# Moving GpSimd's elementwise work to VectorE in a retention + two-FFN kernel, with the second layer's loads and operands re-timed

## The chip, the cores and the metric

One core of a Trainium2 chip runs the whole program. The metric is the device time of one execution in microseconds, as the median of several runs. Engines are named as in the profile: PE (TensorE matmul), PEld (its weight load), DVE (VectorE), ACT (ScalarE), POOL (GpSimd), SP (SyncE, which issues nearly all transfers here).

## What is computed

The reference is a retention layer (attention without softmax, with a decay mask), followed by two feed-forward layers:

```
scores = scale * q @ k^T                 # 4 batches, 8 heads, 576 positions, head size 64
ret    = (scores * Dmat) @ v             # Dmat[h, i, j] = gamma_h ** (i - j) for i >= j, else 0
x      = tokens(ret)                     # 2304 tokens x 512
h = x @ w_in;  x = max(0.01 * h, h) @ w_out     # layer 1, inner size 2048
h = x @ w_in2; out = (h * cos(h)) @ w_out2      # layer 2, inner size 2048
```

## The kernel before

**Precision.** Each fp32 operand is held as a high part (rounded by ACT) and a low part (the rest, a subtraction on DVE or POOL), and each product is made of three matmuls. The weights arrive as 64-bit words and are converted by ACT and DVE.

**Retention** runs over 18 chunks of 128 tokens. For a chunk `i`: `load_chunk(i)` (SP), `scale_q(i)` and `scale_v(i)` (elementwise, 128x512), `scores(i)` (PE, L255), `masks(i)` (DVE, L271), `values(i)` (PE, L286 and L300), `states(i)` (DVE, L318 and L320), `reads(i)` (PE, L333), `take(i)` (ACT, L359). Chunks alternate between two buffers, so chunk `i + 2` is loaded after `reads(i)`.

**Layer 1** runs over five blocks of tokens (512, 512, 512, 384, 384) and 16 tiles `f` of the inner size. A step issues `H(j, f)` on PE (`h_mm`, L456), and, two steps late (`LAG = 2`), `O(j, f)` (`o_mm`, L470). Between the two the result goes through ACT, ACT and DVE (L737, L741, L744). The chunks of block `j + 1` are worked on between the steps of block `j`. The block's input is split into high and low by `split_block` (ACT L675, DVE L679) once the last `H` of the block before has read the old one.

**Block 0** is written out by hand, and every engine takes its instructions in the order of the text. In the same steps DVE converts the layer's weights: in step `s` it does `conv_b` and `conv_c` for the weight tile two steps ahead (L402, L404, L408, L415) and, between them, `low_of(s + 1)` (L427), the low half of the next step's weight tile. Tiles 0 to 14 are converted whole, tile 15 in two halves. At the end of the step come

```
            if i is not None:
                reads(i)
                take(i)
                load_chunk(i + 2)
                if i + 2 >= n_busy:
                    scale_q(i + 2)
                    scale_v(i + 2)
```

with `n_busy` = 8. Chunks 4 to 7 are read in steps 4, 7, 10 and 13, so chunks 8 and 9 are loaded and scaled at the end of steps 10 and 13. They are first used in block 1.

**Blocks 1 to 4 and layer 2** are put in order by a planner (`Plan`): each task has an engine, an estimated time, what it needs and a due time; the planner plays the tasks through and writes each engine's instructions in the order that it found. On the chip each engine keeps to that order and waits where a task isn't ready. During blocks 1 to 4 the second layer's operands are made and stored in DRAM: weights by `second_weights` (converting, L931 to L942; sums, L837; splits, L816 and L820) and the tokens' combinations by `x_parts` (load L856, four sums on L837, four splits on L816 and L820). For token blocks 1 and 2 of layer 2, `x_parts` runs while layer 2 already does block 0.

**Layer 2** uses seven products in place of eight for 2x2 blocks. 24 units `u`; in each PE does `i_mm` (L1056) for `m` in the order 1, 5, 6, 2, 7, 3, 4 and, interleaved and later, `out_` (L1185). Results of `m` = 1 and 6 are copied by ACT from bank to bank (L1158); `gate` makes h * cos(h) with five DVE and five ACT steps (L1085 to L1122).

`low_switch` hands the memory of the first `EARLY` weight tiles to the second layer and begins its loads, `open_all` hands over the rest after the last `O`.

Of the kernel before, what the change touches and what calls it, by code (L numbers as in the profile page):

```python
# [19 lines left out]
P = 128  # L20
# [20 lines left out]
FIRST_CHUNK = 4  # L41
EARLY = 6

# [31 lines left out]

LATE, DRAIN = 12, 6
N_G, N_WO, N_H = 16, 4, 6

# [5 lines left out]
class Plan:  # L84
# [4 lines left out]
    def __init__(self):  # L89
        self.tasks = []  # L90
        self.rings = {}

    def add(self, eng, ns, emit, needs=(), due=0.0, lands=0, frees=()):

        self.tasks.append([eng, ns, emit, needs, due, lands, frees])
        return len(self.tasks) - 1

    def taken(self, ring, size):

        tiles = self.rings.setdefault(ring, [])  # L100
        old = tiles[-size] if len(tiles) >= size else []
        tiles.append([])
        return old, tiles[-1]

    def play(self):
        n = len(self.tasks)
        after = [[] for _ in range(n)]
        left = [0] * n
        for t, task in enumerate(self.tasks):
            for d in {*task[3], *task[6]} - {None}:  # L110
                after[d].append(t)
                left[t] += 1
        ready = [0.0] * n
        free = {}
        open_ = {t for t in range(n) if not left[t]}
        order = []
        self.began = {}
        while open_:

            def begins(t):  # L120
                return max(ready[t], free.get(self.tasks[t][0], 0.0))
# [3 lines left out]
            eng, ns, _, _, _, lands, _ = self.tasks[t]  # L125
            start = begins(t)
            free[eng] = start + ns
            open_.remove(t)
# [23 lines left out]
def retention_ffn_ffn(  # L152
# [67 lines left out]
    def scale_q(i):  # L220
        q = ch_t[i][:, 0]

        eng = nc.vector if i < n_busy else nc.gpsimd
        eng.tensor_tensor(out=q, in0=q, in1=itab_sb, op=ALU.mult)

    def scale_v(i):
        c = i % CYCLE * H
        if i in (1, 2) or n_first <= i < n_busy:
            for h in range(H):
                v = ch_t[i][:, 3, h * D : (h + 1) * D]  # L230
                nc.scalar.activation(v, v, AF.Copy, scale=vtab_sb[:, c + h : c + h + 1])
            return
        v3 = ch_t[i][:, 3].rearrange("p (h d) -> p h d", h=H)
        t3 = vtab_sb[:, c : c + H].unsqueeze(2).to_broadcast([P, H, D])
        eng = nc.gpsimd if i else nc.vector
        eng.tensor_tensor(out=v3, in0=v3, in1=t3, op=ALU.mult)
# [307 lines left out]
    def rest():  # L544
# [53 lines left out]
        for s in range(NF, len(steps) + LAG):  # L598
            i = chunk_at.get(s)
            o = steps[s - LAG]  # L600
            if s < len(steps):
                slots.append(("H", *steps[s]))
                if i is not None:
                    slots.append(("values", i))
                if s + 1 in chunk_at:
                    slots.append(("scores", chunk_at[s + 1]))
            if o[0]:
                slots.append(("O", *o))
            if i is not None:
                slots.append(("reads", i))  # L610
# [44 lines left out]

        SOON = 1000.0
        ACT = {128: 300, 256: 400, 384: 510, 512: 625}
        DVE = {128: 250, 256: 420, 384: 560, 512: 690}
        POOL = {256: 700, 512: 1320}

        def dma(ns, emit, needs, due, frees=()):
            return add("SP", ns, emit, needs, due, 2500, frees)

# [4 lines left out]
        def split_block(j, due):  # L668
            x_ready[j] = []
            n = TB[j]  # L670
            for p in range(KK):
# [10 lines left out]

                a = add("ACT", ACT[n], x_high, [x_use.get((j - 1, p)), *taken[j]], due + p / 100 - SOON)
                x_ready[j].append(add("DVE", DVE[n], x_low, [a], due + p / 100 - SOON))

# [35 lines left out]
        def ffn_h(slot):  # L721
# [28 lines left out]
            t = add("ACT", ACT[n], high, [t], due - SOON / 2, 0, g.old)  # L750
            t = add("DVE", DVE[n], lower, [t], due - SOON / 2)
            y.users.append(t)
# [26 lines left out]
        def chunk(i):  # L779
            due = at["scores", i]  # L780
            if i not in scaled:
                t = dma(2800, lambda: load_chunk(i), read_of[i - 2], due - 12)
                a = add("POOL", POOL[512], lambda: scale_q(i), [t], due - 4)
                b = add("POOL", POOL[512], lambda: scale_v(i), [t], due - 2)
                scaled[i] = [a, b]
# [22 lines left out]

        def split(src, buf, n, to_high, to_low, needs, due, eng="POOL"):

# [18 lines left out]
            h_ = add("ACT", ACT[n], high, needs, due, 0, old)  # L829
            l_ = add(eng, (POOL if eng == "POOL" else DVE)[n], lower, [h_], due)  # L830
            t = dma(1400 * n // 512, store, [l_], due)
# [7 lines left out]
        def sums(eng, first, ops, frees, due, n=256):  # L839
# [3 lines left out]
            for x, op in enumerate(ops):  # L843
                t = [add(eng, (POOL if eng == "POOL" else DVE)[n], lambda op=op: less(e, *op), t, due, 0, frees if not x else ())]
            return t[0]
# [3 lines left out]
        def x_parts(n, q, due, early_=True):  # L849

            bufs, got = (s_ring.next(), s_ring.next()) if early_ else tuple(Use(b) for b in pair_buf), []
            for l in range(2):
# [18 lines left out]
            made = sums(  # L871
                "POOL", got[0] + got[1],
                [(t1, b12, b11, sub_), (t2, b22, t1, sub_), (t3, b22, b12, sub_), (t4, b21, t2, sub_)],
# [21 lines left out]
        def w_sums(p, a11, a12, a21, a22, got, due):  # L895
# [4 lines left out]
            made = sums(  # L900
                "POOL", got,
                [(s1, a21, a22, ALU.add), (s2, s1, a11, sub_), (s3, a11, a21, sub_), (s4, a12, s2, sub_)],
# [15 lines left out]
        def convert(f, c, tb, due, old):  # L918
# [28 lines left out]
            a2 = add("ACT", 430, lambda: nc.scalar.mul(lo().bitcast(I32), lo(), 2.0**-29), [t], due)  # L947
            t = add("DVE", 330, lambda: both(3), [a1], due)
            t = add("DVE", 330, lambda: both(4), [t], due)
            t = add("DVE", 450, lambda: both(5), [t], due)  # L950
            t = add("DVE", 450, lambda: both(6), [t, a2], due)
            rb.users.append(t)
# [45 lines left out]
        def open_low():  # L998
# [5 lines left out]
            some(pool, "ws", [P, 2, 4, 2 * P], F32R, ws_ring.bufs)  # L1004
            some(pool, "wo", [P, 2, 2, DM], F32R, wo_ring.bufs[:3])

# [21 lines left out]

        def add_weights(u):
            p = u % NPAIR  # L1030
            for kind, ring, src, ns in (
                ("a", wa_ring, wa_d, 2100), ("s", ws_ring, ws_d, 2800), ("o", wo_ring, wo_d, 2800),
            ):
                b = w_buf[kind, u] = ring.next()
                w_task[kind, u] = dma(
                    ns, lambda b=b, src=src: nc.sync.dma_start(b.ap.bitcast(F32), src[p]),
                    [opened["all" if kind == "o" and u == 3 else "low"], *w_there[kind, p]],
                    unit_at(u) - (16 if kind != "o" else 4), b.old,
                )
# [3 lines left out]
        def add_x(n):  # L1043
            for x, m in enumerate(ORDER):
                b = x_now[m] = Use(x_buf[m])
                x_task[n, m] = dma(
                    2100, lambda m=m, b=b: nc.sync.dma_start(b.ap.bitcast(F32), xq_d[n][:, X_OF[m]]),
                    [opened["low"], *parts_done[n]], unit_at(NPAIR * n) - 12 + x, b.old,
                )
# [26 lines left out]
        def gate(u, m, due):  # L1076
# [27 lines left out]

            t = add("DVE", 560, rest_a, [t], due, 0, rb.old)
            t = add("DVE", 560, rest_b, [t], due)
            nb.users.append(t)
# [7 lines left out]

            t = add("DVE", 560, times, [t], due)
            rb.users.append(t)
# [7 lines left out]

            t = add("DVE", 560, lower, [t], due)
            hb.users.append(t)
# [126 lines left out]
        for slot in slots:  # L1254
# [3 lines left out]
            if slot == ("O", NB - 1, NF - 1):  # L1258
                first_banks()
                opened["all"] = add("-", 0, open_all, [*busy["a"], *busy["b"], opened["low"]], 0)  # L1260
        for _, _, fn in flows:
# [163 lines left out]
```

## Time and profile before

| | |
|---|---|
| median of 3 runs | 884.04 us (882.31 to 887.03) |
| profiled execution | 880.0 us, of which the span of the instructions is 878.2 us |
| busy: PE, PEld | 848.1 us (97%), 777.7 us (89%) |
| busy: DVE, ACT, POOL | 581.3 us (66%), 519.2 us (59%), 194.4 us (22%) |
| mean granted TensorE clock | 0.988 |

Retention's start and the first weights take the first 40 to 60 us; layer 1 runs to 493 us, layer 2 from there to 874.5 us. A timeline row gives start, length, engine, line, operation, output and inputs, count and, in brackets, how long the engine was idle before it and what ended that.

### The profile page before, as it was taken

The page shows a single profiled execution, that of the slowest core. Times are in us where ns is not written, and L with a number is a line of the kernel's source. Part 1 is how long each engine was busy: PE and PEld are TensorE (multiplying, and loading weights), DVE is VectorE, ACT ScalarE, POOL GpSimd, SP SyncE. Part 2 cuts the span into 40 slices and gives each one's busy share as a digit, 9 for nine tenths or more (in the row PEclk, how much of TensorE's full clock was granted, in tenths as well). Part 3 has the DMA queues.
Part 4 walks back from the last instruction along what each step waited for, and adds up shares of the span by engine and source line. Part 5 has one row for each costly group of instructions (what it writes and reads, how often), then busy time and mean ns, then how long its engine had stood idle before and what let it go on. Part 6 is the DMA issues. An engine that isn't in the chain of part 4 may idle for free.

```text
span 878.2 us, 16385 instructions
## 1 busy us (share of the span) xinstructions
PE 848.1 (97%) x6288; PEld 777.7 (89%) x6288; DVE 581.3 (66%) x1015; ACT 519.2 (59%) x1112; POOL 194.4 (22%) x177
## 2 busy tenths in 40 slices
PE   6699999999999999999999999999999999999998
PEld 6577888777787887989999999999999999999998
DVE  5799975566674557454721377888787776765772
ACT  4687764454555445445632478686778665777650
POOL 0000021453435436363320123413323000000000
PEclk8799999999999999999999999999999999999999
DMA  9915422655557665754469486989999398474311
GB/s 362 417 58 203 178 74 84 217 180 191 176 175 240 192 216 165 247 174 163 174 242 416 139 283 191 321 303 395 311 315 324 134 373 318 150 273 180 132 48 73
DMA packets 91950, 193.31 MB, mean 220 GB/s; under 512 B 7648, under 2 KB 55264, under 8 KB 81632
## 3 DMA queue, kind: packets, MB, share of 16 engines
q1 hardware_dynamic: 91728, 191.92, 62.2%
q8 instruction: 49, 0.80, 0.4%
q10 hardware_dynamic: 144, 0.35, 0.1%
q14 instruction: 29, 0.24, 0.1%
HBM read 143.22 MB, written 49.02 MB: 219 GB/s over the span
## 4 chain that ended last, share of the span: by engine, by line
PE 71%; DVE 12%; DMA 9%; ACT 4%; issue 2%; POOL 1%; SPq 1%; DVEq 0%; ACTq 0%; POOLq 0%
PE psum L1185 19%; PE psum L470 17%; PE psum L456 16%; PE psum L1056 15%; DMA raw<-in_w 2%; DMA mraw<-in_w 2%; PE psum L333 2%; DVE g L1122 1%; DMA wo<-more 1%; DVE r L1096 1%; DMA ws<-mt 1%; DVE r L1101 1%; PE psum L255 1%; DMA ch<-in_qkv 1%; PE psum L286 1%
## 5 line engine op out<-in xcount | busy, mean ns | idle before, releaser
L456 PE MATMUL psum<-x_sb,w 128*128 128x512 f32 (+1 forms) x960 | 218.2, 376 | 6.7 <-DVE x_sb L679 2.8
L1185 PE MATMUL psum<-g,wo 128*128 128x384 f32 x1152 | 222.4, 334 | 0.0
L470 PE MATMUL psum<-g,w 128*128 128x512 f32 (+1 forms) x960 | 215.3, 373 | 0.3 <-ACT graw L700 0.3
L456 PEld LDWEIGHTS psum<-x_sb,w 128*128 128x128 f32 x960 | 176.9, 191 | 34.1 <-DVE x_sb L679 4.6
L1185 PEld LDWEIGHTS psum<-g,wo 128*128 128x128 f32 x1152 | 201.7, 188 | 0.0
L470 PEld LDWEIGHTS psum<-g,w 128*128 128x128 f32 x960 | 173.9, 188 | 24.8 <-ACT graw L700 0.6
L1056 PE MATMUL psum<-x,ws 128*128 128x384 f32 x576 | 115.1, 335 | 4.4 <-ACT psum L1158 4.4
L1056 PEld LDWEIGHTS psum<-x,ws 128*128 128x128 f32 x576 | 100.8, 188 | 6.3 <-ACT psum L1158 6.3
L744 DVE TENSOR_TENSOR g<-graw,g 128x512 fp32r<-128x512 f32 (+1 forms) x64 | 44.2, 691 | 80.8 <-ACT g L741 80.6
L1056 PE MATMUL psum<-x,wa 128*128 128x384 f32 x432 | 86.3, 334 | 0.2 <-DVE h L1085 0.2
L1122 DVE TENSOR_TENSOR g<-h,g 128x384 fp32r<-128x384 f32 x96 | 60.4, 630 | 26.8 <-ACT g L1119 26.5
L1056 PEld LDWEIGHTS psum<-x,wa 128*128 128x128 f32 x432 | 75.9, 188 | 0.5 <-DVE h L1085 0.5
L1112 DVE SCALAR_TENSOR_TENSOR h<-r,h 128x384 f32<-128x384 f32 x96 | 55.6, 580 | 27.0 <-ACT r L1109 26.7
L741 ACT CAST g<-graw 128x512 fp32r<-128x512 f32 (+1 forms) x64 | 36.1, 564 | 57.2 <-PE psum L470 56.9
L1096 DVE SCALAR_TENSOR_TENSOR r<-n,h 128x384 f32<-128x384 int32 x96 | 59.0, 615 | 13.2 <-ACT n L1093 12.6
L1108 ACT ACTIVATE r<-r 128x384 f32<-128x384 f32 x96 | 50.5, 526 | 28.5 <-DVE r L1101 28.0
L737 ACT ACTIVATE graw<-psum 128x512 f32<-128x512 f32 (+1 forms) x64 | 34.7, 542 | 47.9 <-PE psum L456 47.7
L1101 DVE SCALAR_TENSOR_TENSOR r<-n,r 128x384 f32<-128x384 int32 x96 | 58.2, 607 | 1.7
L1093 ACT ACTIVATE n<-h 128x384 int32<-128x384 f32 x96 | 49.3, 519 | 11.6 <-DVE h L1085 11.2
L1119 ACT CAST g<-h 128x384 fp32r<-128x384 f32 x96 | 49.1, 512 | 10.5 <-DVE h L1112 10.3
L1109 ACT ACTIVATE r<-r 128x384 f32<-128x384 f32 x96 | 50.4, 525 | 2.0
L837 POOL TENSOR_TENSOR m<-m 128x256 f32<-128x256 f32 x24 | 22.0, 935 | 122.2 <-DMA m<-y 121.8
(81 smaller groups left out, 936.9 us busy)
## 6 DMA issues: line engine op xcount, KB each, us to landing
ws<-ws SPq DMA_DIRECT2D x24, 1024.0 KB, 7.0
wo<-wo SPq DMA_DIRECT2D x24, 1024.0 KB, 5.6
wa<-wa SPq DMA_DIRECT2D x24, 768.0 KB, 6.6
ch<-in_qkv SPq DMA_DIRECT2D x17, 1024.0 KB, 7.0
mraw<-in_w SPq DMA_DIRECT2D x64, 256.0 KB, 3.4
x<-xq SPq DMA_DIRECT2D x21, 768.0 KB, 8.8
raw<-in_w SPq DMA_DIRECT2D x15, 1024.0 KB, 10.0
xq<-m SPq DMA_DIRECT2D x84, 128.0 KB, 4.5
```

Of the source, the lines that this page charges most:

```text
L456: nc.tensor.matmul(hp, wt[:, i, cols], x_t[lj, k][:, j, :n], start=(k == 0 and a == 0), stop=(k == KK - 1 and a == 2),)
L470: nc.tensor.matmul(psum[:, BANK_O + m, :n], wt[:, i, cols], gt[:, j, :n], start=(f == 0 and a == 0), stop=(f == NF - 1 and a == 2),)
L1056: nc.tensor.matmul(bank[BANKS[m]], a[:, hl, i, j * P : (j + 1) * P], x[:, j, v, :], start=m in (1, 5) and j == 0 and n == 0, stop=j == 1 a ...
L1093: t = add("ACT", 515, lambda: nc.scalar.activation(n_ap(), hb.ap, AF.Copy, scale=INV_2PI), [t], due, 0, nb.old)
L1096: nc.vector.scalar_tensor_tensor(out=r_ap(), in0=n_ap(), scalar=-C1, in1=hb.ap, op0=ALU.mult, op1=ALU.add)
L1101: nc.vector.scalar_tensor_tensor(out=r_ap(), in0=n_ap(), scalar=-C2, in1=r_ap(), op0=ALU.mult, op1=ALU.add)
L1108: t = add("ACT", 515, lambda: nc.scalar.activation(r_ap(), r_ap(), AF.Sin, scale=0.5), [t], due)
L1109: t = add("ACT", 515, lambda: nc.scalar.activation(r_ap(), r_ap(), AF.Square), [t], due)
L1112: nc.vector.scalar_tensor_tensor(out=hb.ap, in0=r_ap(), scalar=0.5, in1=hb.ap, op0=ALU.subtract, op1=ALU.mult)
L1119: t = add("ACT", 515, lambda: nc.scalar.copy(gb.ap[:, 0], hb.ap), [t], due, 0, gb.old)
L1122: nc.vector.tensor_tensor(out=gb.ap[:, 1], in0=hb.ap, in1=gb.ap[:, 0].bitcast(F32), op=ALU.subtract)
L1185: nc.tensor.matmul(bank[m], wt[:, i, hl, m * P : (m + 1) * P], gt[:, v, :], start=h == 0 and z == 0 and x == 0, stop=h == 1 and z == 1 and ...
```

## The change

All elementwise work of GpSimd goes to VectorE, except `scale_v` of chunk 3: the scaling of chunks 8 to 17, all sums and all splits. At each block change from block 1 on, `O` of the old block's tile 14 is issued before `H` of the new block's tile 0 (before: after it). `EARLY` goes from 6 to 4; of the second layer's `wo` buffers one (before: three) lies in the memory that is opened early, and the next are loaded after `open_all`. `x_parts` for the second layer's token blocks 1 and 2 moves from units 2, 3, 4 and 8, 9, 10 to units 1, 3, 5 and 8, 11, 14. The planner counts SP's time 5% longer, second-layer loads as landing in 3500 ns (before: 2500), and VectorE's two-input work and GpSimd's as excluding each other.

```diff
-EARLY = 6
+EARLY = 4
...
+LANDS = 3500
...
     def scale_q(i):
         q = ch_t[i][:, 0]
 
-        eng = nc.vector if i < n_busy else nc.gpsimd
-        eng.tensor_tensor(out=q, in0=q, in1=itab_sb, op=ALU.mult)
+        nc.vector.tensor_tensor(out=q, in0=q, in1=itab_sb, op=ALU.mult)
...
-        eng = nc.gpsimd if i else nc.vector
+        eng = nc.gpsimd if 0 < i < n_first else nc.vector
...
             o = steps[s - LAG]
-            if s < len(steps):
-                slots.append(("H", *steps[s]))
...
-            if o[0]:
-                slots.append(("O", *o))
+            if s % NF == 0 and o[0]:
+                slots += [("O", *o), *new]
+            else:
+                slots += new
+                if o[0]:
+                    slots.append(("O", *o))
...
-        def dma(ns, emit, needs, due, frees=()):
-            return add("SP", ns, emit, needs, due, 2500, frees)
+        def dma(ns, emit, needs, due, frees=(), lands=2500):
+            return add("SP", LOAD * ns, emit, needs, due, lands, frees)
...
-                a = add("POOL", POOL[512], lambda: scale_q(i), [t], due - 4)
-                b = add("POOL", POOL[512], lambda: scale_v(i), [t], due - 2)
+                a = dve(DVE[512], lambda: scale_q(i), [t], due - 4)
+                b = dve(DVE[512], lambda: scale_v(i), [t], due - 2)
...
-        def split(src, buf, n, to_high, to_low, needs, due, eng="POOL"):
+        def split(src, buf, n, to_high, to_low, needs, due, eng="DVE"):
...
             made = sums(
-                "POOL", got[0] + got[1],
+                "DVE", got[0] + got[1],
...
             made = sums(
-                "POOL", got,
+                "DVE", got,
...
-            some(pool, "wo", [P, 2, 2, DM], F32R, wo_ring.bufs[:3])
+            some(pool, "wo", [P, 2, 2, DM], F32R, wo_ring.bufs[:1])
...
-            for n, u in ((1, 2), (2, 8)):
-                d = at["i", u + q, 1]
+            for n, u in ((1, 1 + 2 * q), (2, 8 + 3 * q)):
+                d = at["i", u, 1]
...
             add_x(0)
-            for u in range(3):
-                add_weights(u)
+            for u in range(2):
+                add_weights(u, "as" if u else "aso")
+
+        def all_switch():
+            opened["all"] = add("-", 0, open_all, [*busy["a"], *busy["b"], opened["low"]], 0)
+            add_weights(1, "o")
+            add_weights(2)
```

## Rows read from the trace of the kernel before

**Rows 1.** The page's first part: busy us, share of the span, instructions.
```profile
PE 848.1 (97%) x6288; PEld 777.7 (89%) x6288; DVE 581.3 (66%) x1015; ACT 519.2 (59%) x1112; POOL 194.4 (22%) x177
```

**Rows 2.** Windows: length, busy time and count by engine, clock, DMA.
```profile
320.00:340.00 20.00, 17.93 (x90) 14.35 (x87) 11.82 (x19) 10.26 (x24) 11.21 (x10) 1.00 0.64 207
...
500.00:520.00 20.00, 17.34 (x99) 16.70 (x98) 14.75 (x25) 15.98 (x34) 6.53 (x6) 1.00 0.84 286
...
340.20:343.70 3.50, 3.50 (x12) 3.16 (x11) 3.43 (x8) 2.31 (x5) 1.53 (x1) 0.51 0.40 121
336.80:340.20 3.40, 1.33 (x6) 0.85 (x6) 3.40 (x7) 0.99 (x3) 1.49 (x1) 1.00 0.58 172
```

**Rows 3.** Timeline of PE, 200 to 400 us.
```profile
240.94 0.97 PE L456 MATMUL psum<-x_sb,w 128*128 128x512 f32 x3 [0.74 <-DVE x_sb L679]
...
338.28 0.80 PE L456 MATMUL psum<-x_sb,w 128*128 128x384 f32 x3 [1.32 <-DVE x_sb L679]
339.83 2.93 PE L456 MATMUL psum<-x_sb,w 128*128 128x384 f32 x9 [0.75 <-DVE x_sb L679]
...
388.55 1.15 PE L333 MATMUL psum<-ch,st 64*64 64x64 f32 x32 [2.12 <-DVE st L320]
```

**Rows 4.** Waits: waiting engine and line, releaser: us, times, longest.
```profile
PE psum L1056 <- ACT psum L1158: 4.4, 6, 1.4
```

**Rows 5.** Window of line 820 alone on POOL: the splits.
```profile
0.00:880.00 880.00, 110.77 (x84) 0.99 0.63 220
```

**Rows 6.** Window of line 837 alone on POOL: the sums.
```profile
0.00:880.00 880.00, 57.52 (x68) 0.99 0.63 220
```

**Rows 7.** Lines of DVE by form: count, busy us, mean ns, idle before.
```profile
L320 DVE TENSOR_TENSOR st<-psum,st 128x256 f32<-128x256 f32 x28 | 11.8, 421 | 9.4 <-PE psum L300 5.5 <-PE psum L333 2.2 <-DVE st L320 0.5
...
L224 DVE TENSOR_TENSOR ch<-ch,tabs_sb 128x512 f32<-128x512 f32 x8 | 5.5, 687 | 6.2 <-DMA tabs_sb<-in_tabs 5.5 <-DMA ch<-in_qkv 0.7
```

**Rows 8.** Timeline of DVE, 96 to 142 us.
```profile
103.03 0.69 DVE L402 TENSOR_SCALAR t<-t 128x1024 f32<-128x1024 f32 x1
...
104.36 1.22 DVE L427 TENSOR_TENSOR w<-t,w 128x1024 fp32r<-128x1024 f32 x1
...
110.53 1.75 DVE L404 TENSOR_SCALAR t<-t 128x1024 uint32<-128x1024 uint32 x1
112.21 2.06 DVE L427 TENSOR_TENSOR w<-t,w 128x1024 fp32r<-128x1024 f32 x1
...
123.30 0.69 DVE L427 TENSOR_TENSOR w<-t,w 128x512 fp32r<-128x512 f32 x1
```

**Rows 9.** Timeline of POOL, 95 to 200 us.
```profile
110.44 1.29 POOL L224 TENSOR_TENSOR ch<-ch,tabs_sb 128x512 f32<-128x512 f32 x1 [90.34 <-DMA ch<-in_qkv]
111.69 1.50 POOL L236 TENSOR_TENSOR ch<-ch,tabs_sb 128x512 f32<-128x512 f32 x1
130.07 1.29 POOL L224 TENSOR_TENSOR ch<-ch,tabs_sb 128x512 f32<-128x512 f32 x1 [16.88 <-DMA ch<-in_qkv]
```

**Rows 10.** Timeline of PE, 58 to 200 us.
```profile
110.66 2.88 PE L456 MATMUL psum<-x_sb,w 128*128 128x512 f32 x12
...
123.81 1.15 PE L333 MATMUL psum<-ch,st 64*64 64x64 f32 x32
...
130.46 2.88 PE L456 MATMUL psum<-x_sb,w 128*128 128x512 f32 x12
```

**Rows 11.** Timeline of DVE, 376 to 392 us.
```profile
380.39 1.31 DVE L931 TENSOR_SCALAR mraw<-mraw 128x256 f32<-128x256 f32 x1 [0.99 <-POOL ch L236]
...
387.56 0.94 DVE L320 TENSOR_TENSOR st<-psum,st 128x256 f32<-128x256 f32 x2
```

**Rows 12.** Timeline of DVE, 486 to 535 us.
```profile
511.11 1.64 DVE L1101 SCALAR_TENSOR_TENSOR r<-n,r 128x384 f32<-128x384 int32 x1
```

**Rows 13.** Timeline of SP, 440 to 700 us: first transfers of a token block.
```profile
596.73 1.20 SPq L856 DMA_DIRECT2D m<-y  x2
```

**Rows 14.** Timeline of POOL, 440 to 640 us: the sums behind that.
```profile
606.74 3.92 POOL L837 TENSOR_TENSOR m<-m 128x256 f32<-128x256 f32 x4 [29.65 <-DMA m<-y]
```

More of the change, by code (lines that the diff above doesn't have):

```diff
@@ L90, in __init__, with add @@
         self.tasks = []
-        self.rings = {}
-    def add(self, eng, ns, emit, needs=(), due=0.0, lands=0, frees=()):
-        self.tasks.append([eng, ns, emit, needs, due, lands, frees])
+    def add(self, eng, ns, emit, needs=(), due=0.0, lands=0, frees=(), port=False):
+        self.tasks.append([eng, ns, emit, needs, due, lands, frees, port or eng == "POOL"])
         return len(self.tasks) - 1
[L98 to L103, printed above, removed]
     def play(self):
@@ L120, in begins @@
             def begins(t):
-                return max(ready[t], free.get(self.tasks[t][0], 0.0))
+                at = max(ready[t], free.get(self.tasks[t][0], 0.0))
+                return max(at, free.get("port", 0.0)) if self.tasks[t][7] else at
             t0 = min(begins(t) for t in open_)
             t = min((x for x in open_ if begins(x) <= t0 + 1), key=lambda x: (self.tasks[x][4], x))
-            eng, ns, _, _, _, lands, _ = self.tasks[t]
+            eng, ns, _, _, _, lands, _, port = self.tasks[t]
             start = begins(t)
             free[eng] = start + ns
+            if port:
+                free["port"] = start + ns
             open_.remove(t)
@@ L599, in rest @@
             i = chunk_at.get(s)
-            o = steps[s - LAG]
-            if s < len(steps):
-                slots.append(("H", *steps[s]))
[L603 to L606, printed above, removed]
-            if o[0]:
-                slots.append(("O", *o))
+            new = []
+            if s < len(steps):
+                new.append(("H", *steps[s]))
+                if i is not None:
+                    new.append(("values", i))
+                if s + 1 in chunk_at:
+                    new.append(("scores", chunk_at[s + 1]))
+            o = steps[s - LAG]
+            if s % NF == 0 and o[0]:
[4 more added lines that the diff above has]
+                    slots.append(("O", *o))
             if i is not None:
@@ L653, in unit_at @@
             return at["i", min(u, n_unit - 1), 1] + max(0, u - n_unit + 1) * 15.6
-        SOON = 1000.0
+        SOON, LOAD = 1000.0, 1.05
         ACT = {128: 300, 256: 400, 384: 510, 512: 625}
@@ L659, in rest, with dve @@
         POOL = {256: 700, 512: 1320}
-        def dma(ns, emit, needs, due, frees=()):
-            return add("SP", ns, emit, needs, due, 2500, frees)
+        def dma(ns, emit, needs, due, frees=(), lands=2500):
+            return add("SP", LOAD * ns, emit, needs, due, lands, frees)
+        def dve(ns, emit, needs, due, frees=()):
+            return add("DVE", ns, emit, needs, due, 0, frees, True)
         x_ready, taken = {}, {j: [] for j in range(NB)}
@@ L683, in split_block @@
                 a = add("ACT", ACT[n], x_high, [x_use.get((j - 1, p)), *taken[j]], due + p / 100 - SOON)
-                x_ready[j].append(add("DVE", DVE[n], x_low, [a], due + p / 100 - SOON))
+                x_ready[j].append(dve(DVE[n], x_low, [a], due + p / 100 - SOON))
         y_stored = {b: [] for b in range(NT // SB)}
@@ L750, in ffn_h @@
             t = add("ACT", ACT[n], high, [t], due - SOON / 2, 0, g.old)
-            t = add("DVE", DVE[n], lower, [t], due - SOON / 2)
+            t = dve(DVE[n], lower, [t], due - SOON / 2)
             y.users.append(t)
@@ L829, in split @@
             h_ = add("ACT", ACT[n], high, needs, due, 0, old)
-            l_ = add(eng, (POOL if eng == "POOL" else DVE)[n], lower, [h_], due)
+            l_ = add(eng, (POOL if eng == "POOL" else DVE)[n], lower, [h_], due, port=True)
             t = dma(1400 * n // 512, store, [l_], due)
@@ L843, in sums @@
             for x, op in enumerate(ops):
-                t = [add(eng, (POOL if eng == "POOL" else DVE)[n], lambda op=op: less(e, *op), t, due, 0, frees if not x else ())]
+                t = [add(eng, (POOL if eng == "POOL" else DVE)[n], lambda op=op: less(e, *op), t, due, 0, frees if not x else (), True)]
             return t[0]
@@ L947, in convert @@
             a2 = add("ACT", 430, lambda: nc.scalar.mul(lo().bitcast(I32), lo(), 2.0**-29), [t], due)
[L948 to L951, printed above, removed]
+            t = dve(330, lambda: both(3), [a1], due)
+            t = dve(330, lambda: both(4), [t], due)
+            t = dve(450, lambda: both(5), [t], due)
+            t = dve(450, lambda: both(6), [t, a2], due)
             rb.users.append(t)
@@ L1027, in rest, with add_weights @@
         w_buf, w_task = {}, {}
-        def add_weights(u):
+        def add_weights(u, kinds="aso"):
             p = u % NPAIR
@@ L1033, in add_weights @@
             ):
+                if kind not in kinds:
+                    continue
                 b = w_buf[kind, u] = ring.next()
@@ L1036, in add_weights @@
                     ns, lambda b=b, src=src: nc.sync.dma_start(b.ap.bitcast(F32), src[p]),
-                    [opened["all" if kind == "o" and u == 3 else "low"], *w_there[kind, p]],
-                    unit_at(u) - (16 if kind != "o" else 4), b.old,
+                    [opened["all" if kind == "o" and u else "low"], *w_there[kind, p]],
+                    unit_at(u) - (16 if kind != "o" else 4), b.old, LANDS,
                 )
@@ L1047, in add_x @@
                     2100, lambda m=m, b=b: nc.sync.dma_start(b.ap.bitcast(F32), xq_d[n][:, X_OF[m]]),
-                    [opened["low"], *parts_done[n]], unit_at(NPAIR * n) - 12 + x, b.old,
+                    [opened["low"], *parts_done[n]], unit_at(NPAIR * n) - 12 + x, b.old, LANDS,
                 )
@@ L1103, in rest_b @@
                 )
-            t = add("DVE", 560, rest_a, [t], due, 0, rb.old)
-            t = add("DVE", 560, rest_b, [t], due)
+            t = dve(600, rest_a, [t], due, rb.old)
+            t = dve(560, rest_b, [t], due)
             nb.users.append(t)
@@ L1114, in times @@
                 )
-            t = add("DVE", 560, times, [t], due)
+            t = dve(560, times, [t], due)
             rb.users.append(t)
@@ L1124, in lower @@
                 )
-            t = add("DVE", 560, lower, [t], due)
+            t = dve(560, lower, [t], due)
             hb.users.append(t)
@@ L1259, in rest @@
                 first_banks()
-                opened["all"] = add("-", 0, open_all, [*busy["a"], *busy["b"], opened["low"]], 0)
+                all_switch()
         for _, _, fn in flows:
```

## The prediction, made before the changed kernel ran

> **What bounds the kernel now.** I read the page's first part, then the windows of 20 us, then PE's timeline wherever a window shows PE short of 20, then the waits, and last the other engines' timelines around each gap.
>
> PE is the bound: 97% busy [rows 1], and after the first 60 us nearly every window is full. So nothing that VectorE or GpSimd does is worth anything by itself; a change pays only by closing PE's gaps, and costs by opening new ones. The gaps from block 1 on are few, and can be listed whole. At the change from block 1 to 2: 0.74 us, waiting for VectorE's split of x. From 2 to 3: 1.32 and 0.75 us for the same, and just behind them TensorE's clock is granted at 0.51 (the lower of its two levels, 1.2 GHz) for 3.5 us, so about half of that, 1.7 us, is lost too. At 388 us: 2.12 us for `states` [rows 2, 3]. In layer 2: 4.4 us in six waits for the bank copy on ACT [rows 4]. Smaller ones (0.26 at 206 us, 0.31 at 354 us, 0.2 in layer 2) make some 0.8. The sum is 11.8 us: all that the change can win in the stages that the planner orders. The rest of the time before is PE's own work, which the change leaves alone.
>
> **Part 1: GpSimd's work on VectorE, amount.** 84 splits [rows 5] and 68 sums [rows 6] move, and by the code 20 scalings (chunks 8 to 17, two each). A two-input 128x512 operation takes VectorE 0.687 us, a 256-wide one 0.421 [rows 7] (from the row with a PSUM input, the nearest). So 84 x 0.687 + 68 x 0.421 + 20 x 0.687 = 58 + 29 + 14 = 100 us, a little less since some splits are narrower. On top of 581 us [rows 1] that is 681 us, 78% of the span, if nothing comes back. VectorE does not become the bound by load.
>
> Something does come back: while GpSimd worked at 110.4 to 113.2 us, VectorE's L404 and L427 took 1.75 and 2.06 us in place of 0.69 (L402, the same size) and 1.22 [rows 8, 9]. GpSimd's 2.8 us cost VectorE 1.9 us; the same two scalings on VectorE cost it 1.4. Where the two overlap, the move makes VectorE quicker. In layer 2 a 0.55 us step (L1101) took 1.64 us [rows 12].
>
> The Trainium skill (SBUF — State Buffer, section "Who interferes with whom") says that a VectorE instruction with two SBUF inputs is locked out for the whole length of a GpSimd instruction that reads SBUF. By that rule the overlap above would have cost up to the full 2.8 us; the trace's 1.9 is less, and the price by the row is what counts here.
>
> **Part 2: chunks 8 and 9 in block 0, the largest term.** This order is by hand, and the diff leaves the place of the two scalings: right behind `load_chunk`. On GpSimd the wait for the transfer (90.34 us of idleness, harmless) held up nobody. On VectorE the scaling stands ahead of the next step's weight conversion, and everything behind it waits for the transfer.
>
> Chunk 8: in step 11 VectorE now begins L402 at 103.03 and ends L427, the low half of tile 12, at 105.58: 2.55 us later. H(0, 12) starts on PE at 110.66 [rows 8, 10]. So the lead is 5.1 us. After: chunk 8 is there at 110.44 [rows 9]; two scalings take 1.3 us (0.69 each, starts 0.6 apart), then the 2.55: 114.3. H(0, 12) starts 3.6 us late.
>
> In between, VectorE runs behind PE until step 13: chunk 7's scaling, `states(7)` and the low halves come just in time or late. I reckon 1.3 us of waits for `scores(7)` and `reads(7)` (0 to 1.5).
>
> Chunk 9: `reads(7)` starts at 123.81, and the chunk is there at 130.07, 6.3 us later [rows 9, 10]. After, from that start: 6.3, two scalings 1.3, two half-size passes 0.85 and L427 at half size 0.69 [rows 8]: 9.1 us. Now H(0, 15) starts at 130.46, 6.65 us behind `reads(7)`. So 2.4 us more.
>
> Together 7.3 us (6 to 8.7), straight onto PE's line, since the weights' low halves are wanted by the next matmul. The clock: the stretch 336.8 to 340.2, in which PE worked 1.33 of 3.4 us, was followed by the lower level [rows 2]; 2.12 us of idleness at 388 was not. An idle 3.6 us is longer than either, so I add one fall, 1.7 us (0 to 3.4). Sum +9.0.
>
> **Part 3: O of tile 14 ahead of H of the new block.** One O is 2.7 us of matmuls in front of the split of x (2.1 after the 384-wide blocks). The gaps it must cover are 0.74 and 2.07 us with the slow clock behind: −0.74 −2.07 −1.7 = −4.5. It covers both with room, the more as the splits were drawn out by GpSimd. What is late next: O's g of tile 14, which loses one H of cover; it still has three groups of matmuls, 8 us, for three operations. Taken −4.3 (−4.5 to −2).
>
> **Part 4: the reads and layer 2.** At 388 us VectorE first waited for GpSimd's scaling (0.99 us), then ran drawn-out conversions (1.31 us for the first), and `states` came behind them [rows 11]. Without GpSimd this should mostly go: −1.6 of 2.12, and −0.4 of the small ones. In layer 2, part of the six waits comes from VectorE's drawn-out steps [rows 12] which hold up ACT and so the bank copy; the longest but one comes behind a table load of ACT that stays. Taken −2.5 of 4.6 (−4.6 to 0).
>
> **Part 5: what adds nothing.** The earlier start of layer 2's loads: PE goes from layer 1 to layer 2 without a gap now, so there is nothing to win; the `wo` loads that become later are wanted only by the first L1185 of unit 1, some 30 us after the switch. The new units for `x_parts` spread 16 operations each, about 4.4 us of VectorE, over units of 16 us and more.
>
> **Part 6: new waits of VectorE in the planned stages.** Every load that GpSimd waited for is now waited for by VectorE, with the g chain and the gates behind it. Lower bound 0 (the planner never reaches a load before it lands). Upper bound from a row: the tokens' transfer issued at 596.73 lands so late that the sums begin at 606.74 [rows 13, 14], 10 us, where the planner reckons some 4; 6 us of VectorE standing still could reach PE there, and once more elsewhere. I take +2, nearer to nothing, because most transfers in layer 1 have 6 us and more of slack behind them on PE.
>
> **Sum.** +9.0 −4.3 −2.0 −2.5 +2 = +2.2 us. Against the profiled execution: 880.0 + 2.2 = 882.2 us. That execution lies 4.0 us below the median of 884.04, so the forecast as a median is 886 us.
>
> **Rivals.**
>
> *Slower, clearly.* Part 6 at its upper bound: VectorE's fixed order meets late transfers in the planned stages, at unit 8 of layer 2 above all, where the seven loads of x go ahead of the tokens' transfer. For it: the 10 us [rows 13, 14]. Against: the planner now counts loads as longer. It decides once VectorE stands for more than about 2 us, for a result read from PSUM there is wanted by PE two products later. Price 9 (6 to 10) in place of 2: 886 + 7 = 893 us.
>
> *Faster.* The shared access of GpSimd and VectorE is the cause of all the late steps in planned stages, and with GpSimd idle all 11.8 us go, no new wait comes, and the clock holds in block 0: 7.3 − 11.8 = −4.5, so 879 to 880 us. For it: each of the long gaps has drawn-out VectorE steps ahead of it. Against: the table load, and ACT's own waits for transfers, which stay. It decides where the gaps left after block 0 come under 3 us in all. The Trainium skill (GPSIMD Engine Reference, section "Engine selection") gives elementwise work to VectorE, as about twice as fast; the trace agrees with 1.29 against 0.69 us. By that rule alone this rival comes out; it says nothing of what waits behind a transfer.
>
> *Slack in block 0.* If the order in block 0 turned out to have slack that I don't see (chunk 8's transfer 5 us earlier), the change would give only the gains, 884.0 − 4.3 − 2.0 − 2.5 + 2 = 877 us; nothing supports it, since the transfer starts when `reads` of chunk 6 has ended, and this is unchanged.
>
> **How the numbers follow.** The forecast case, −2 to +6 us about its +2.2: 0.52. The slower rival: 0.22. The faster one: 0.22. Slack in block 0: 0.04. About 0.5%, 4.4 us, is what a measurement of this kernel can tell from no change. Faster by more: most of the faster rival and the slack, 0.20. Slower by more: the slower rival and the upper quarter of the forecast case, 0.34. The same: 0.46. The range leaves out the tails of both rivals: 878 to 894 us; the forecast case's own is 882 to 890.
>
> **What would show it.** Right: PE gaps ahead of L456 at about 110 and 135 us, ended by VectorE's L427, with VectorE idle for a transfer of `ch` before them (some 7 and 5 us); no gap ahead of L456 with DVE L679 as its releaser; L931, L1096 and L1101 all near their undisturbed length; VectorE near 600 us in all. Wrong: no wait of VectorE for `ch` in block 0, or PE gaps in the planned stages of more than 8 us (the slower rival), or under 3 (the faster).

## The result and the profile after

The change made the kernel faster: 875.16 us (median of 4 runs, 874.54 to 877.37) against 884.35 us, ratio 0.990 (0.987 to 0.993). A second measurement of the same pair gave 875.32 against 881.83 us, ratio 0.993 (0.991 to 0.995). The forecast was 886 us (878 to 894), a little slower: wrong.

The page's first part, after (columns as in [rows 1]):

```profile
PE 847.6 (97%) x6288; PEld 779.3 (89%) x6288; DVE 601.1 (69%) x1187; ACT 518.7 (59%) x1112; POOL 1.7 (0%) x5
```

VectorE does 172 instructions more and is busy only 20 us longer, not 100: its steps are no longer drawn out. Two lines (min/median/max in ns, first and last start) show it, in each pair the kernel before first and the changed one second:

```profile
L931 DVE TENSOR_SCALAR mraw<-mraw x46: 278/294/1380, 143.2 to 447.3; 128x256 f32<-128x256 f32 x46
L935 DVE TENSOR_SCALAR mraw<-mraw x46: 282/286/297, 153.0 to 443.3; 128x256 f32<-128x256 f32 x46
```
```profile
L1096 DVE SCALAR_TENSOR_TENSOR r<-n,h x96: 540/551/1646, 499.9 to 851.0; 128x384 f32<-128x384 int32 x96
L1102 DVE SCALAR_TENSOR_TENSOR r<-n,h x96: 546/550/559, 500.9 to 848.6; 128x384 f32<-128x384 int32 x96
```

Block 0 went nearly as forecast. VectorE's timeline after (answers [rows 8, 9]; L219 is `scale_q`, L422 `low_of`):

```profile
110.27 0.69 DVE L219 TENSOR_TENSOR ch<-ch,tabs_sb 128x512 f32<-128x512 f32 x1 [8.54 <-DMA ch<-in_qkv]
...
112.81 1.22 DVE L422 TENSOR_TENSOR w<-t,w 128x1024 fp32r<-128x1024 f32 x1
...
135.95 0.69 DVE L219 TENSOR_TENSOR ch<-ch,tabs_sb 128x512 f32<-128x512 f32 x1 [7.54 <-DMA ch<-in_qkv]
...
137.96 0.68 DVE L422 TENSOR_TENSOR w<-t,w 128x512 fp32r<-128x512 f32 x1
```

PE's timeline after (answers [rows 10]; L451 is H):

```profile
114.08 5.06 PE L451 MATMUL psum<-x_sb,w 128*128 128x512 f32 x11 [4.42 <-DVE w L422]
...
138.70 3.98 PE L451 MATMUL psum<-x_sb,w 128*128 128x512 f32 x11 [2.01 <-DVE w L422]
```

And the windows behind these two waits (the column after POOL's is the granted clock):

```profile
114.08:118.90 4.82, 4.82 (x11) 3.47 (x11) 4.75 (x7) 4.68 (x9) 0.00 (x0) 0.50 0.00 0
118.90:122.80 3.90, 3.90 (x46) 3.12 (x46) 3.87 (x5) 2.94 (x9) 0.00 (x0) 0.92 0.00 0
...
138.70:142.50 3.80, 3.80 (x12) 2.98 (x13) 3.13 (x5) 1.14 (x2) 0.00 (x0) 0.68 0.02 4
142.50:146.00 3.50, 3.50 (x15) 2.85 (x14) 0.00 (x0) 0.67 (x2) 0.00 (x0) 0.86 0.00 0
```

VectorE stands still for 8.5 and 7.5 us, PE waits 4.4 and 2.0 us, and TensorE's clock falls to its lower level twice. Yet the gaps of [rows 3] are gone. PE's timeline at the change to block 3 shows 24 matmuls of O in one row and H behind it with nothing in brackets; the wait for `states` has shrunk to 0.62 us:

```profile
341.83 5.61 PE L465 MATMUL psum<-g,w 128*128 128x512 f32 x24
347.28 2.99 PE L451 MATMUL psum<-x_sb,w 128*128 128x384 f32 x16
```
```profile
370.12 1.15 PE L328 MATMUL psum<-ch,st 64*64 64x64 f32 x32 [0.62 <-DVE st L315]
```

To set runs side by side I cut each PE timeline at the same matmuls: the first of H(0, 12), of H(1, 1) (both orders have done O of the old tile 14 by then), and of units 0, 4, 8 and 16. Stretches in us, from one profile each; from unit 16 to the end of the last matmul all are alike (145.8):

```
                  to H(0,12)  block 0   blocks 1-4   units    units   units
                              rest      to unit 0    0-3      4-7     8-15
before               110.7     33.8      349.0       41.7     68.3    125.3
before_again         110.7     33.8      350.9       41.7     68.0    125.3
after                109.3     44.9      340.7       39.1     67.6    124.8
after_again          110.9     44.4      340.6       38.9     67.6    124.8
pool89               111.1     33.8      340.7       38.9     67.6    124.8
late                 111.0     33.8      340.8       38.3     67.6    124.8
allpool              111.3     33.8      340.2       44.3     67.6    125.8
late_oldchange       111.6     33.8      340.8       38.7     67.6    124.8
b_engine             111.4     33.7      343.0       39.6     71.4    124.9
b_change             109.4     33.8      352.2       41.0     68.2    125.4
b_port               111.3     33.8      342.0       39.5     75.8    133.0
late_oldfigures      110.0     33.8      342.0       39.5     67.6    124.8
late_early6          110.6     33.8      341.2       39.7     67.6    124.8
late_oldunits        110.7     33.8      340.9       38.2     70.6    132.6
units_figures        111.2     33.8      340.6       38.4     72.0    128.2
units_early          111.3     33.8      340.6       39.3     67.6    127.0
```

Before to after: block 0 loses 11.1 us, blocks 1 to 4 win 8.3, layer 2 wins 3.8. The first column, 109.3 to 111.6 over all profiles, shows how far a stretch varies by itself.

### The profile page after: what moved, and what is told of

The parts are those of the page before. It is cut to its first block, busy times and chain, and to the rows that moved or that the text cites. A ratio compares the mean times of both kernels' runs of the same rounds, so it can differ in the third digit from the quotient of the medians.

```text
span 875.6 us, 16272 instructions
## 1 busy us (share of the span) xinstructions
PE 847.6 (97%) x6288; PEld 779.3 (89%) x6288; DVE 601.1 (69%) x1187; ACT 518.7 (59%) x1112; POOL 1.7 (0%) x5
## 4 chain that ended last, share of the span: by engine, by line
PE 84%; DMA 7%; DVE 6%; issue 1%; ACT 1%; SPq 0%; DVEq 0%; ACTq 0%
PE psum L1191 22%; PE psum L465 19%; PE psum L451 19%; PE psum L1062 19%; DMA ch<-in_qkv 4%; PE psum L328 2%; PE psum L250 1%; PE psum L281 1%; DMA mraw<-in_w 1%; PE psum L295 1%; DMA xq<-m 1%; DVE w L422 1%; DVE t L410 1%; DVE t L403 1%; DMA ws<-ws 1%
## 5 line engine op out<-in xcount | busy, mean ns | idle before, releaser
L451 PE MATMUL psum<-x_sb,w 128*128 128x512 f32 (+1 forms) x960 | 218.4, 377 | 10.6 <-DVE w L422 7.2
L451 PEld LDWEIGHTS psum<-x_sb,w 128*128 128x128 f32 x960 | 177.3, 191 | 37.5 <-DVE w L422 8.3
L748 DVE TENSOR_TENSOR g<-graw,g 128x512 fp32r<-128x512 f32 (+1 forms) x64 | 39.9, 624 | 68.4 <-ACT g L745 67.7
L1118 DVE SCALAR_TENSOR_TENSOR h<-r,h 128x384 f32<-128x384 f32 x96 | 52.9, 553 | 24.5 <-ACT r L1115 24.2
L1102 DVE SCALAR_TENSOR_TENSOR r<-n,h 128x384 f32<-128x384 int32 x96 | 52.9, 551 | 11.9 <-ACT n L1099 11.6
L1128 DVE TENSOR_TENSOR g<-h,g 128x384 fp32r<-128x384 f32 x96 | 52.6, 552 | 11.1 <-ACT g L1125 10.4
L1107 DVE SCALAR_TENSOR_TENSOR r<-n,r 128x384 f32<-128x384 int32 x96 | 53.1, 553 | 1.6
L1210 DVE SCALAR_TENSOR_TENSOR acc<-psum,acc 128x384 f32<-128x384 f32 x48 | 26.7, 556 | 16.4 <-PE psum L1191 15.3
```

Of the source, the lines that this page charges most:

```text
L451: nc.tensor.matmul(hp, wt[:, i, cols], x_t[lj, k][:, j, :n], start=(k == 0 and a == 0), stop=(k == KK - 1 and a == 2),)
L1102: nc.vector.scalar_tensor_tensor(out=r_ap(), in0=n_ap(), scalar=-C1, in1=hb.ap, op0=ALU.mult, op1=ALU.add)
L1107: nc.vector.scalar_tensor_tensor(out=r_ap(), in0=n_ap(), scalar=-C2, in1=r_ap(), op0=ALU.mult, op1=ALU.add)
L1118: nc.vector.scalar_tensor_tensor(out=hb.ap, in0=r_ap(), scalar=0.5, in1=hb.ap, op0=ALU.subtract, op1=ALU.mult)
L1128: nc.vector.tensor_tensor(out=gb.ap[:, 1], in0=hb.ap, in1=gb.ap[:, 0].bitcast(F32), op=ALU.subtract)
```

## The experiments

My theory after the result: block 0 costs about 10 us, and the engine change wins more than that behind it, since GpSimd drew out VectorE's steps. The rival: the new order at the block changes and the planner's new figures closed the gaps. First, the kernel before once more.

**before_again** (no edit).

> The kernel before, unchanged, profiled a second time. Theory A (its executions differ, and the first profiled one, 880.0 us, was a short one): about 884 us, with 2 to 5 us more of PE gaps in blocks 1 to 4 or at the start of layer 2 than the first profile has, in other places. Rival B (the executions are alike on PE and the time lies outside the gaps): about 880 us, the same gaps within 1 us.

881.68 us, like its neighbours' median on that chip (881.61). Its gaps are larger than the first profile's, in the same places; from PE's timeline:

```profile
339.48 1.84 PE L456 MATMUL psum<-x_sb,w 128*128 128x384 f32 x9 [2.50 <-DVE x_sb L679]
...
354.98 1.46 PE L470 MATMUL psum<-g,w 128*128 128x384 f32 x5 [1.79 <-ACT graw L700]
```

The gap of 0.31 us at 354 us is now 1.79. So neither theory whole: blocks 1 to 4 are 1.9 us longer, but in the same places, and the time is 881.68 us and not 884. One profile of the kernel before shows its gaps some 2 us smaller than the other.

**pool89** and **late.** Two ways to take the wait out of block 0: GpSimd scales chunks 8 and 9 again, or VectorE does so when they have long landed.

```diff
+        eng = nc.gpsimd if i in (n_busy, n_busy + 1) else nc.vector      # pool89, scale_q; scale_v alike
...
-                if i + 2 >= n_busy:                                       # late
-                    scale_q(i + 2)
-                    scale_v(i + 2)
+            if s >= NF - 2:
+                scale_q(n_busy + s - NF + 2)
+                scale_v(n_busy + s - NF + 2)
```

> The changed kernel with the scaling of chunks 8 and 9 back on GpSimd, all else as changed. Theory A (the two waits of VectorE for chunks 8 and 9 and the slow clock behind them cost about 10 us in block 0): 10 us under the changed kernel, about 865 us, no PE gap ahead of L451 or its like in block 0 after 60 us, H(1,0) some 10 us earlier. Rival B (later stages would absorb what block 0 loses, or block 0 is held by something else): 0 to 3 us under the changed kernel.

> The changed kernel with the scaling of chunks 8 and 9 still on VectorE but at the end of steps 14 and 15, when the transfers have long landed. Theory A (the wait is what costs, not the engine): as with the scaling on GpSimd or up to 2 us better, 863 to 866 us. Rival B (VectorE is so full in block 0 that any extra work shows on PE): 2 to 5 us worse than with the scaling on GpSimd.

867.49 us, ratio 0.983 (0.982 to 0.985), and 867.00 us, ratio 0.983 (0.981 to 0.984). Both have block 0 back at 33.8 us. VectorE does the scaling in `late` without any wait in front:

```profile
126.05 0.68 DVE L219 TENSOR_TENSOR ch<-ch,tabs_sb 128x512 f32<-128x512 f32 x1
126.65 0.68 DVE L231 TENSOR_TENSOR ch<-ch,tabs_sb 128x512 f32<-128x512 f32 x1
```

So it was the wait that cost, not the work. `late` has the lowest median of this study, though pool89, and late_oldchange below, can't be told from it.

**after_again** (the changed kernel, beside the others).

> The changed kernel itself, on one chip with the runs beside it. Theory A (block 0 costs what the traces show, 7.2 us of late weights and about 4 behind them with the slow clock): about 0.9 to 1.1% above the kernels that scale chunks 8 and 9 elsewhere or later, so a ratio to before of 0.992 to 0.995. Rival B (the first ratio, 0.990, holds, and block 0 costs only some 6 us in untraced runs): 0.989 to 0.991.

Ratio 0.993, theory A. Against `late`, 0.983: 1.0% or some 9 us for the two waits and the slower clock behind them, where the profiles say 10.6 (44.4 to 33.8). Both profiled executions of the changed kernel were the longest of their sets (877.37, 878.06); why is open.

**allpool.** The changed kernel with sums, splits and scaling back on GpSimd; `sums` and the scalings from chunk 8 on are changed in the same manner.

```diff
-        def split(src, buf, n, to_high, to_low, needs, due, eng="DVE"):
+        def split(src, buf, n, to_high, to_low, needs, due, eng="POOL"):
...
```

> The changed kernel with all of GpSimd's work back on GpSimd (sums, splits, scalings from chunk 8 on), the changed order of O at the block changes, the planner's figures and the units of the operands kept. Theory A (the engines' contention made the gaps of the planned stages): gaps of several us come back in layer 2 and at reads, and the time is some 8 us above the two kernels that have VectorE do it without waiting, 872 to 876 us. Rival B (the order at the block changes and the planner's new figures closed the gaps, the engine does not matter): within 2 us of those two, about 865 us.

874.35 us, ratio 0.991 (0.990 to 0.993): 7 us above `late`. But not where I expected it. Blocks 1 to 4 are as short as ever (340.2); 6 of the 7 us are one gap in unit 0 and the slower matmuls after it, behind operands that are made later on GpSimd: the last of their stores is issued at 467 us, in `late` at 436, and the loads of x follow from 470 on, three of seven only at 487:

```profile
493.94 4.04 PE L1063 MATMUL psum<-x,ws 128*128 128x384 f32 x12 [4.36 <-DMA x<-xq]
```

So moving the work is not the only cure for the blocks: with the new plan GpSimd may do it too.

**b_change** and **late_oldchange.** The order at the block changes, alone and taken out.

```diff
+            first_ = s % NF == 0 and o[0]       # b_change: before, O ahead of H
+            if first_:
+                slots.append(("O", *o))
...
-            if s % NF == 0 and o[0]:            # late_oldchange: late, H ahead of O
+            if False:
```

> The kernel before with the new order at the block changes alone. Theory A (the split of x is the wait that sets those gaps, and one O covers it): the 0.74 us at the change to block 2 and the 2.1 us with the slow clock at the change to block 3 go, 3 to 5 us faster, ratio 0.994 to 0.997. Rival B (O of tile 14 comes too early for its g, so the gap moves behind it): within 1 us of before.

> The changed kernel with chunks 8 and 9 scaled late, and with the old order at the block changes (H of the new block's tile 0 ahead of O of tile 14). Theory A (the new order closes the gaps ahead of the split of x): gaps of about 1 us at the change to block 2 and 2 to 4 us at the change to block 3 come back, ratio to before 0.986 to 0.989 in place of 0.983. Rival B (with VectorE's steps no longer drawn out, the split of x is in time in either order): 0.982 to 0.984, no gap with x_sb as releaser.

Ratio 0.999 (0.998 to 1.001) and 0.983 (0.981 to 0.986): both times rival B. Alone, the new order moves the gap from x to g of tile 14. PE and DVE of b_change, at the change to block 3:

```profile
336.78 4.33 PE L470 MATMUL psum<-g,w 128*128 128x512 f32 x12 [2.40 <-DVE g L747]
```
```profile
332.25 0.29 DVE L934 TENSOR_SCALAR mraw<-mraw 128x256 f32<-128x256 f32 x1 [2.92 <-ACT mraw L948]
...
334.97 1.75 DVE L747 TENSOR_TENSOR g<-graw,g 128x512 fp32r<-128x512 f32 x1
```

VectorE waits for a conversion on ACT, then runs four conversion steps, three of them drawn out (0.72, 0.84 and 0.84 us; in the changed kernel their lines take 0.29, 0.42 and 0.42), and the low half of g takes 1.75 us in place of 0.69. In `late_oldchange` the old order has no gap there: once VectorE is in time, neither order matters.

**b_engine.** The kernel before with the engine change alone, chunks 8 and 9 left on GpSimd.

> The kernel before with the engine change alone, in the planned stages: sums, splits and the scaling of chunks 10 to 17 on VectorE, chunks 8 and 9 left on GpSimd, the planner's figures as before. Theory A (GpSimd's contention draws out VectorE's steps and so makes most gaps of the planned stages): 5 to 9 us faster, ratio 0.990 to 0.994, the start of layer 2 some 3 us shorter. Rival B (the engine alone brings new waits of VectorE for transfers and gains nothing without the planner's new figures): within 3 us of before, gaps of 2 us and more at unit 8 or at reads.

869.99 us, ratio 0.986 (0.984 to 0.989): 12 us, theory A and more. Blocks 1 to 4 come to 343.0, units 0 to 3 to 39.6. Units 4 to 7 lose 3: ACT waits for stores of operands (twice, 1.41 and 1.56 us), and the bank copy behind it is late. ACT and PE there:

```profile
566.36 0.62 ACT L816 CAST m<-m 128x512 fp32r<-128x512 f32 x1 [1.56 <-DMA xq<-m]
```
```profile
569.24 2.03 PE L1056 MATMUL psum<-x,ws 128*128 128x384 f32 x6 [1.89 <-ACT psum L1158]
```

**b_port.** The kernel before; only the planner knows that GpSimd's and VectorE's two-input work exclude each other.

> The kernel before with one thing changed: the planner counts GpSimd's work and VectorE's two-input SBUF work as excluding each other, GpSimd still does its work. Theory A (blocks 1 to 4 lost time because the order was planned without the contention; a plan that knows of it avoids it): blocks 1 to 4 some 6 to 10 us shorter, as in the kernel with all else changed and the work on GpSimd, ratio 0.988 to 0.993. Rival B (that kernel's gain came from the other new figures or the order of O): within 3 us of before.

Theory A for the blocks: they come to 342.0, 7 to 9 us shorter. But the plan doesn't avoid the contention: the conversions are drawn out as before. The line of L931, here L936, has the same mean (484 ns; 485 before, 288 in the changed kernel). The first row is of the kernel before, the second of b_port:

```profile
L931 DVE TENSOR_SCALAR mraw<-mraw 128x256 f32<-128x256 f32 x46 | 22.3, 485 | 37.6 <-ACT mraw L945 30.9 <-issue 5.5 <-POOL ch L236 1.0
L936 DVE TENSOR_SCALAR mraw<-mraw 128x256 f32<-128x256 f32 x46 | 22.2, 484 | 21.1 <-ACT mraw L950 16.1 <-DMA xq<-mt 3.1 <-DMA mraw<-in_w 1.4
```

What the plan changes is the order, and by it the blocks are shorter with the steps as long as before. And units 4 to 15 lose 15 us, which neither theory foresaw: layer 2's waits of PE are now for h on VectorE (7.8 us, 4 times) and for the bank copy (5.7 us, 3 times). The whole is slower: 890.19 us, ratio 1.009 (1.006 to 1.012).

**late_oldfigures**, **late_early6**, **late_oldunits.** The planner's figures, the start of layer 2's loads, and the units of `x_parts`, each put back in `late`.

```diff
-        SOON, LOAD = 1000.0, 1.05               # late_oldfigures, with LANDS = 2500, first gate step 560 (600 in the change)
+        SOON, LOAD = 1000.0, 1.0
...
-            for n, u in ((1, 1 + 2 * q), (2, 8 + 3 * q)):       # late_oldunits
+            for n, u in ((1, 2 + q), (2, 8 + q)):
```

> The changed kernel with chunks 8 and 9 scaled late, and with the planner's old figures (SP's time as before, loads landing in 2500 ns everywhere, the first gate step 560 ns). Theory A (VectorE meets late transfers unless the planner counts loads as longer): PE gaps of 1 to 3 us come back in blocks 1 to 4 or layer 2, ratio 0.985 to 0.988. Rival B (with VectorE's steps at their undisturbed length the planner's order is good enough either way): 0.982 to 0.984.

> The changed kernel with chunks 8 and 9 scaled late, and the second layer's loads begun two tiles later again (EARLY 6, three wo buffers early). Theory A (the operands are made 15 us earlier with VectorE, so the start of the loads is not on PE's path): within 1 us, ratio 0.982 to 0.984. Rival B (the earlier start pays): 1 to 4 us longer at the start of layer 2.

> The changed kernel with chunks 8 and 9 scaled late, and x_parts back at units 2, 3, 4 and 8, 9, 10. Theory A (operands crowded into neighbouring units make ACT and VectorE wait for buffers, as in the engine change alone, where units 4 to 8 took 3.3 us longer): units 4 to 8 take 2 to 4 us longer, ratio to before 0.985 to 0.987 in place of 0.983. Rival B (the planner's new figures prevent that by themselves): 0.982 to 0.984, units 4 to 8 within 0.5 us.

Ratios 0.987 (0.984 to 0.990), 0.985 (0.982 to 0.988) and 0.993 (0.990 to 0.996), against 0.983 (0.981 to 0.984). The figures are worth 2 to 4 us (near theory A, with gaps of 0.7 to 1.1 us); the earlier loads at most 2, too little for these intervals. The units are worth 9, more than either theory said. With the old units PE waits for weights whose load SP issued only at 650.74. By the chain that the profile follows, it stood behind a load of tokens, and that one behind a store of operands that was still landing; the chain, then PE:

```profile
645.12 5.02 DMA xq<-m
...
650.16 0.52 SPq L860
...
650.74 8.91 DMA ws<-ws
```
```profile
659.70 2.29 PE L1062 MATMUL psum<-x,ws 128*128 128x384 f32 x6 [4.99 <-DMA ws<-ws]
```

**units_figures** and **units_early.** With the old units, also the old figures, or the old start of the loads.

> Chunks 8 and 9 scaled late, x_parts at the old units and the planner's old figures together. With the new figures the old units cost 11 us in units 4 to 16, with the engine change alone (old units, old figures, old start of the loads) only 3.8. Theory A (the new figures, which make SP's plan longer, turn crowded operands into late weight loads): units 8 to 16 back within 1 us of 124.8, units 4 to 8 still 2 to 4 us longer, ratio to before 0.986 to 0.990. Rival B (the figures play no part in that): units 8 to 16 still 5 us or more longer, ratio 0.992 to 0.996.

> Chunks 8 and 9 scaled late, x_parts at the old units, the loads of layer 2 begun as late as before (EARLY 6, three wo buffers early), the planner's new figures. Theory A (the figures are what turns crowding into late loads): as with the old units alone, units 8 to 16 some 7 us longer, ratio 0.991 to 0.996. Rival B (the fewer early wo buffers leave more loads to the crowded stretch): units 8 to 16 within 2 us of 124.8, ratio 0.984 to 0.988.

Ratios 0.991 (0.988 to 0.994) and 0.987 (0.985 to 0.990). Units 4 to 15 take 200.2 and 194.6 us, with the old units alone 203.2, with the new ones 192.4. Neither theory holds whole: both parts raise the price of crowded operands, the start of the loads more. So the crowded units cost 2 to 11 us, as the other parts stand; which transfers push which was followed only in the chain above.

## Why the prediction was wrong

The step that failed is the size of the gain behind block 0. Parts 3, 4 and 6 put it at −6.8 us in all; the first two profiles show −12.1. Part 3 gave the gaps at the block changes to the order, Part 4 only a part of the others to GpSimd, and Part 6 added waits of VectorE that didn't reach PE. The engine change alone (b_engine) is worth 12 us by its ratio.

**Part 1, right.** VectorE did not become the bound, and beside GpSimd its steps were drawn out. The 100 us for the moved work were right too: it takes 95 us after (55.1 for the splits, 26.1 for the sums, 20 scalings of 0.69). What came back was larger than I took into the sum: VectorE's other work takes 75 us less.

**Part 2, right in the mechanism, a little short.** The two waits come to 6.4 us, for 6.0 forecast; the 1.3 between them didn't come. The term of the wrong size is the clock: it fell twice. By the granted clock of the four windows above the falls cost some 4.4 us, not 1.7. Together the profiles say 11.1 us in place of 9.0. Taken out, it is worth 9 us.

**Part 3, the wrong step.** I gave the gaps at the block changes to the missing cover of one O. The order alone brings nothing (0.999); the split was late because VectorE and ACT were, and g of tile 14, for which I reckoned 8 us of cover, was just as late. What closes the gaps is VectorE in time: by the engine (b_engine), or by a plan that counts the contention (b_port), though its steps stay drawn out there. In the changed kernel both are changed; either is enough.

**Part 4, too small.** The reads and layer 2's start were put down as −4.5; blocks 1 to 4 won 8.3 us in place of the 6.3 of Parts 3 and 4 together, layer 2 3.8 in place of 2.5.

**Part 5, the second wrong step.** The spread units were put at nothing, by their load alone. With `late` they are worth 9 us beside the other parts. The old units bring much of the slower rival's loss, in the units from 8 on, though in `late_oldunits` it is the weights' load that is late and not VectorE. So Parts 5 and 6 belong together: that Part 6 came to nothing is in part the spread units' work. It is shown for `late`; the changed kernel itself was not run with the old units.

**Part 6, wrong.** Put at +2; in the changed kernel VectorE waited for tokens' loads 0.9 us in all. For chunks it waited longer:

```profile
DVE ch L219 <- DMA ch<-in_qkv: 27.5, 9, 8.5
...
DVE m L841 <- DMA m<-y: 0.9, 1, 0.9
```

Of these 27.5 us, 16.1 are the two waits in block 0, and 10.2 fall into blocks 1 to 4 (longest 5.6). There PE's one gap over 0.2 us is the 0.62 for `states`: the slack behind the transfers, which I had argued for most of them, covered them all.

**The sum.** I reckoned by profile: +2.2; the two first profiles differ by −2.6 in span (878.2 to 875.6). So 4.8 us of the error lies in the profiles: 2.0 in blocks 1 to 4, 1.3 in layer 2 and 2.0 in Part 6, with block 0 going 2.1 the other way. The rest of it, 1.6, lies in no term: 1.4 is the stretch ahead of H(0, 12), which varies by itself. Some 6 us more of the error is how I went from one profile to medians: 880.0 was short for the kernel before (881.7 in its second profile), so that I added 4.0, and 877.37 was 2.2 long for the changed one. Why the profiled executions lie so far from their medians is open.

The faster rival had the mechanism behind block 0 right, and what it took the gaps to give, 11.8 us, was reached: 8.3 and 3.8 by the stretches. The gaps over 0.2 us left after block 0 are 0.62, 1.25 and 0.58, under the 3 us at which it decided. Only its assumption that the clock holds in block 0 failed.

## What to carry to other kernels

An engine that slows its neighbour costs more than its own idle time shows: before costing a move by its instructions, compare each line's median length with its longest. Drawn-out steps need not reach the bound engine, though: in b_port and allpool they stayed, and the blocks were short. When work moves to an engine that keeps to its order, look for the transfers that the old engine was free to wait for: the scalings of two chunks, 1.3 us each, cost 9 us only for their place, and moving them to the ends of steps 14 and 15 gave that back. And a gap ahead of a wait says who was last, not what would cure it: the order that covered the split of x only showed the next late one. A sum made against one profile carries that profile's own distance from the median; here it was half of the error.

## What the hardware showed that I had not expected

TensorE's clock fell to its lower level (granted 0.50) after PE's wait of 4.42 us and again after the one of 2.01 us (0.68 over the next 3.8 us), while a wait of 2.12 us in the kernel before [rows 3] had left it alone. Nor does the length of the last wait settle it: in before_again the clock stayed at 1.00 behind the wait of 2.50 us and came to 0.58 behind the one of 1.79:

```profile
339.40:343.00 3.60, 3.30 (x16) 2.84 (x17) 3.56 (x9) 2.29 (x5) 0.98 (x1) 1.00 0.47 140
...
354.98:359.00 4.02, 4.02 (x14) 3.98 (x15) 1.77 (x4) 2.23 (x5) 2.49 (x2) 0.58 0.75 228
```

So the two falls in block 0 can't be read from the two waits' lengths alone. GpSimd's elementwise work cost VectorE time beside its own: GpSimd was busy 193 us with it, and with that gone VectorE's other work fell by 75 us (95 us of moved work, 20 us of busy time added).
